# A single-token decode layer: every second weight or cache chunk, but for the last six, loaded from ScalarE's DMA queue

## The chip, the cores and the metric

The kernel runs on one core of a Trainium2 chip. The time is device microseconds (us) of one execution. Most executions of it agree within a few hundredths of a per cent: three runs lie between 229.84 and 229.97 us.

## What is computed

One token `x` (1 x 1024) goes through a layer norm; the result `xn` feeds two branches in parallel, and both are added to `x`.

- Attention with a cache: 32 query heads in 4 groups of 8, each group with its own keys and values. Of 65,536 cached positions only the last 4,096 are read.
- A gated feed-forward with 3,584 hidden columns.

```python
xn = layernorm(x)
q = (xn @ wq)                                   # 1024 -> 32 heads x 128
p = softmax(q . k_cache[last 4096] * 128**-0.5) # per head; 8 heads share one of 4 key groups
attention = (p @ v_cache[last 4096]) @ wo       # 4096 -> 1024
h = gelu(xn @ w_gate) * (xn @ w_up)             # 1024 -> 3584, tanh form of gelu
out = x + attention + h @ w_down                # 3584 -> 1024
```

All is float32. With one token there is hardly any arithmetic per weight: 94.4 MB of weights and cache are read once, and each value is used once (a key or value of the cache eight times).

## The kernel before

**Chunks.** All that is read from memory is cut into 24 chunks, listed in `items` (lines 75 to 79) in the order in which they are used:

`q0 q1 q2 q3 | k0 g0 v0 g1 g2 g3 | k1 u0 v1 u1 u2 u3 | o0 o1 o2 o3 | d0 d1 d2 d3`

The letters stand for `wq` (q), the keys (k) and values (v) of the cache, `w_gate` (g), `w_up` (u), `wo` (o) and `w_down` (d). A chunk fills a tile `chunk` of 128 partitions x 8192 floats (4 MB), or less: a chunk of q or o has one row of 32 KB for each partition, one of g or u has 28 KB for each partition, and one of k or v is two loads (two groups, the first and the second half of the tile) with 16 KB for each partition. d0 and d1 are like o; d2 is loaded in two pieces and d3, half as large, in five (`TAIL`, line 30).

**Four buffers.** The pool `stream` (line 55) has four buffers, and chunk n takes the buffer of chunk n - 4. So the load of chunk n has to wait until all engines are done with chunk n - 4. `load(n)` (line 88) issues the loads of chunk n. The first four are issued at the start; after that the main loop (line 410) works on chunk n and then calls `load(n + 4)` (line 450). All of these loads, lines 104 and 106, are issued by SyncE (SP), whose queue takes them in this order. An engine runs its instructions in the order in which the code emits them, and `manual_schedule` (line 58) leaves that order alone; a load that has to wait for its buffer therefore holds back what stands behind it on the engine that issues it.

**Work on a chunk.**
- q, g, u (`project`, line 201): the first half of each row goes through TensorE (PE, line 196), the second half through VectorE (DVE), which scales it by the token's value and adds it up in `part` (lines 184 and 186). The buffer is free when both are done.
- k (`transpose_keys` and `scores`, lines 235 and 245): for each of two groups of heads PE transposes the keys in eight groups of four blocks (line 241), ScalarE (ACT) moves each of them out of PSUM (line 242), PE forms the scores (line 250), DVE takes the maximum (line 253), and ACT the exponential (line 256). Between the two groups of k0 the queries are finished (lines 211 to 226), and between those of k1 the gelu (lines 344 to 355). The buffer is free after the last transpose of the second group.
- v (`values`, line 261): PE transposes the probabilities, ACT moves them out (line 273), PE multiplies them with the values (line 278).
- o and d (`contract`, line 393): half of the rows on PE (line 389), half on DVE (line 186); for the last chunks all on PE.

ScalarE issues two loads itself, both of `x`, at the start (lines 111 and 114); else it computes.

Of the kernel before, what the change touches and what calls it, by code (L numbers as in the profile page):

```python
# [39 lines left out]
def tile_decode_layer(  # L40
# [12 lines left out]
    nc = tc.nc  # L53
# [21 lines left out]
    items = [("q", jj) for jj in range(NJ)]  # L75
# [12 lines left out]
    def load(n):  # L88
        kind, i = items[n]
        chunk = stream.tile([P, STREAM], F32, name="chunk")  # L90
        at = 0
        for src in source[kind](i):
            size = math.prod(src.shape[1:])
            dst = chunk[:, at:at + size]
            at += size
            if len(src.shape) == 3:
                dst = dst.rearrange("p (t n) -> p t n", t=src.shape[1])
            step = TAIL.get(len(items) - 1 - n)
            if step:
                for t in range(0, src.shape[1], step):  # L100
                    cuts = 2 if n == len(items) - 1 and t == src.shape[1] - 1 else 1
                    for cut in range(cuts):
                        cols = slice(cut * D // cuts, (cut + 1) * D // cuts)
                        nc.sync.dma_start(dst[:, t:t + step, cols], src[:, t:t + step, cols])
            else:
                nc.sync.dma_start(dst, src)
        loaded[kind, i] = chunk


# [296 lines left out]
    for n in range(ahead):  # L406
        load(n)
    layer_norm()
    state = None
    for n, (kind, i) in enumerate(items):  # L410
# [38 lines left out]
        if n + ahead < len(items):  # L449
            load(n + ahead)  # L450
# [27 lines left out]
```

## Time and profile before

| | |
|---|---|
| median of 3 runs | 229.92 us (229.84 to 229.97) |
| the profiled execution | 229.72 us, of which its span is 227.9 us |
| mean granted TensorE clock | 0.79 |
| busy: PE, DVE, ACT | 54%, 43%, 15% of the span |
| DMA: q1 (SyncE's queue) | 97.1% of what 16 engines could work in the span |
| read from HBM | 94.38 MB |

The span runs from the first to the last instruction; the rest of the time, 1.8 us, lies around it. The times in the views of the trace count from the span's start. In a timeline, a row has its start, how long it takes, the engine and line, what is done, and in square brackets how long the engine had been idle and who ended that. SPq and ACTq are the instructions by which SyncE and ScalarE issue loads: what follows such a row is the issue and not the move of the data. Matmuls of float32 show as two records each.

### The profile page before, as it was taken

What the parts mean: (1) busy time and instruction counts of PE and PEld (TensorE: products, weight loads), DVE (VectorE), ACT (ScalarE), POOL (GpSimd) and SP (SyncE); (2) the same over time, 40 slices, a digit from 0 to 9 for tenths busy, and PEclk for the clock granted to TensorE, in tenths of its full rate; (3) what the DMA queues carried; (4) which work ended last, traced back from release to release, by engine and by line L of the source; (5) the groups of instructions that cost most, each with busy time, mean ns of one, the idle gap of its engine ahead of it and who ended that gap; (6) DMA issues with size and microseconds to landing.
All of it is one profiled execution on the core that took longest, in us unless ns stands there. A gap on an engine that the chain in (4) does not pass through costs nothing.

```text
span 227.9 us, 2497 instructions
## 1 busy us (share of the span) xinstructions
PE 123.2 (54%) x1096; PEld 60.6 (27%) x1096; DVE 97.0 (43%) x103; ACT 33.3 (15%) x57; POOL 0.7 (0%) x6
## 2 busy tenths in 40 slices
PE   1160622567679834269806985384875425063754
PEld 1110000144364701017305472110571202021331
DVE  7340724520204164260380227966817356292600
ACT  2000000054273400006316350000000000000000
POOL 1000000000000000000000000000000000000000
PEclk9999999599958996577975899959655556675879
DMA  7989999999999999999999999999999999999991
GB/s 277 455 380 454 460 391 443 411 456 436 393 440 461 410 410 453 401 438 451 400 428 449 428 424 441 428 443 403 440 454 405 437 449 414 431 443 391 436 378 47
DMA packets 4786, 94.53 MB, mean 415 GB/s; under 512 B 540, under 2 KB 552, under 8 KB 1192
## 3 DMA queue, kind: packets, MB, share of 16 engines
q1 hardware_dynamic: 4760, 94.38, 97.1%
q8 instruction: 8, 0.13, 0.2%
q14 instruction: 2, 0.02, 0.0%
q10 hardware_dynamic: 16, 0.01, 0.0%
HBM read 94.38 MB, written 0.00 MB: 414 GB/s over the span
## 4 chain that ended last, share of the span: by engine, by line
DMA 57%; PE 22%; DVE 11%; ACT 6%; issue 2%; SPq 0%; ACTq 0%; DVEq 0%
DMA chunk<-in_A_k_cache 23%; DMA chunk<-in_B_w_down 15%; DMA chunk<-in_A_wo 14%; PE kt_p L241 8%; DMA chunk<-in_A_wq 5%; PE o_p L278 3%; DVE part L186 3%; PE s_p L250 3%; PE out_p L389 3%; PE acc_q L196 2%; DVE out_part L186 2%; DVE m L253 2%; ACT kT L242 2%; ACT p L256 2%; ACT pT L273 1%
## 5 line engine op out<-in xcount | busy, mean ns | idle before, releaser
L186 DVE SCALAR_TENSOR_TENSOR part<-chunk,xz,part 128x3584 f32<-128x3584 f32 (+1 forms) x9 | 37.1, 4126 | 32.1 <-DMA chunk<-in_A_wq 17.8
L241 PE MATMUL kt_p<-ident,chunk 128*128 128x128 f32 x128 | 23.7, 354 | 15.9 <-ACT kT L242 13.1
L242 ACT ACTIVATE kT<-kt_p 128x512 f32<-128x512 f32 x32 | 18.2, 596 | 70.9 <-PE kt_p L241 70.9
L196 PE MATMUL acc_q<-chunk,xz 128*32 128x512 f32 x64 | 14.3, 1043 | 24.0 <-DMA chunk<-in_A_wq 24.0
L241 PEld LDWEIGHTS kt_p<-ident,chunk 128*128 128x128 f32 x128 | 18.6, 180 | 24.8 <-ACT kT L242 16.2
L389 PE MATMUL out_p<-chunk,hz 128*32 128x256 f32 x160 | 14.8, 530 | 16.5 <-DMA chunk<-in_B_w_down 16.5
L186 DVE SCALAR_TENSOR_TENSOR out_part<-chunk,oz,out_part 128x1024 f32<-128x1024 f32 x15 | 19.3, 1285 | 10.4 <-DMA chunk<-in_A_wo 10.0
L389 PE MATMUL out_p<-chunk,oz 128*32 128x256 f32 x128 | 13.1, 580 | 15.7 <-DMA chunk<-in_A_wo 15.7
L196 PE MATMUL acc_g<-chunk,xz 128*32 128x512 f32 x56 | 10.9, 817 | 11.6 <-DMA chunk<-in_B_w_gate 11.6
L253 DVE TENSOR_REDUCE m<-s_p 128x1 f32<-128x1024 f32 x4 | 4.9, 1222 | 22.0 <-PE s_p L250 22.0
L186 DVE SCALAR_TENSOR_TENSOR out_part<-chunk,hz,out_part 128x1024 f32<-128x1024 f32 x8 | 10.3, 1284 | 9.1 <-DMA chunk<-in_B_w_down 8.9
L389 PEld LDWEIGHTS out_p<-chunk,hz 128*32 128x32 f32 x160 | 6.7, 147 | 24.6 <-DMA chunk<-in_B_w_down 12.5
L196 PEld LDWEIGHTS acc_q<-chunk,xz 128*32 128x32 f32 x64 | 2.5, 159 | 34.2 <-DMA chunk<-in_A_wq 23.3
L389 PEld LDWEIGHTS out_p<-chunk,oz 128*32 128x32 f32 x128 | 5.2, 156 | 23.2 <-DMA chunk<-in_A_wo 18.5
L196 PE MATMUL acc_u<-chunk,xz 128*32 128x512 f32 x56 | 9.4, 713 | 2.6 <-DMA chunk<-in_B_w_up 2.6
L278 PE MATMUL o_p<-chunk,pT 128*32 128x128 f32 x256 | 7.8, 274 | 1.9 <-ACT pT L273 1.9
L250 PE MATMUL s_p<-kT,qz 128*32 128x512 f32 x64 | 8.7, 612 | 0.0
L184 DVE TENSOR_SCALAR part<-chunk,xz 128x3584 f32<-128x3584 f32 (+1 forms) x3 | 6.5, 2169 | 3.9 <-DMA chunk<-in_A_wq 3.9
L278 PEld LDWEIGHTS o_p<-chunk,pT 128*32 128x32 f32 x256 | 6.7, 110 | 2.9 <-ACT pT L273 2.9
L196 PEld LDWEIGHTS acc_g<-chunk,xz 128*32 128x32 f32 x56 | 2.1, 133 | 18.9 <-DMA chunk<-in_B_w_gate 14.5
L256 ACT ACTIVATE p<-s_p,negm 128x1024 f32<-128x1024 f32 x4 | 4.5, 1114 | 8.5 <-DVE negm L254 8.5
L350 DVE TENSOR_TENSOR t_sb<-g_sb 128x512 f32<-128x512 f32 (+1 forms) x2 | 1.4, 686 | 9.8 <-ACT g_sb L349 9.8
(93 smaller groups left out, 73.5 us busy)
## 6 DMA issues: line engine op xcount, KB each, us to landing
chunk<-in_A_wq SPq DMA_DIRECT2D x4, 4096.0 KB, 30.8
chunk<-in_A_wo SPq DMA_DIRECT2D x4, 4096.0 KB, 27.6
chunk<-in_B_w_gate SPq DMA_DIRECT2D x4, 3584.0 KB, 20.5
chunk<-in_B_w_up SPq DMA_DIRECT2D x4, 3584.0 KB, 16.5
chunk<-in_A_k_cache SPq DMA_DIRECT2D x4, 2048.0 KB, 28.3
chunk<-in_A_v_cache SPq DMA_DIRECT2D x4, 2048.0 KB, 28.5
chunk<-in_B_w_down SPq DMA_DIRECT2D x2, 4096.0 KB
chunk<-in_B_w_down SPq DMA_DIRECT2D x2, 2048.0 KB, 30.9
```

What stands on the lines that cost most here:

```text
L184: nc.vector.tensor_scalar(total, w, factor, None, op0=ALU.mult)
L186: nc.vector.scalar_tensor_tensor(total, w, factor, total, op0=ALU.mult, op1=ALU.add)
L196: nc.tensor.matmul(acc[kind][32 * c:32 * c + 32, b, :], z, w[:, n * NB:(n + 1) * NB], start=start, stop=stop,)
L241: nc.tensor.transpose(t_p[:, jj * P:(jj + 1) * P], kn[:, j * DH:(j + 1) * DH], ident)
L242: nc.scalar.activation(kT[:, i, :], t_p, AF.Copy)
L250: nc.tensor.matmul(s_p[32 * c:32 * c + 32, b, :], qz[:, g, :], kT[:, i, :], start=True, stop=True)
L253: nc.vector.reduce_max(m[:, g:g + 1], s_p, axis=AX.XY)
L256: nc.scalar.activation(p, s_p, AF.Exp, bias=negm[:, g:g + 1], scale=SCALE, accum_out=l[:, g:g + 1])
L273: nc.scalar.activation(pT[:, b].rearrange("p j q -> p (j q)"), t_p, AF.Copy)
L278: nc.tensor.matmul(o_p[32 * c:32 * c + 32, g, :], pT[:, b, jj, 32 * c:32 * c + 32], vn[:, j * DH:(j + 1) * DH], start=(b == 0 and jj == 0) ...
L350: nc.vector.tensor_mul(ts, gs, gs)
L389: nc.tensor.matmul(out_p[32 * c:32 * c + 32, :], z, w[:, c * CO:(c + 1) * CO], start=start, stop=stop)
```

## The change

`load` picks the issuing engine by the chunk's number: odd ones below 18 go to ScalarE. These are nine chunks: q1, q3, g0, g1, g3, u0, u1, u3 and o1. All others stay with SyncE, the last six (o2, o3 and all of d) among them. Buffers, their number, the order of work on PE and DVE, and the shapes of the loads are the same. The lines of the kernel behind the change stand two further down.

```diff
     def load(n):
         kind, i = items[n]
         chunk = stream.tile([P, STREAM], F32, name="chunk")
+
+        queue = nc.scalar if n % 2 and n < len(items) - 6 else nc.sync
...
             else:
-                nc.sync.dma_start(dst, src)
+                queue.dma_start(dst, src)
```

On SyncE, from its first load to that of `wo`: the rows before are q0 to q3, k0, g0, v0, then g1, g2 and g3, k1, u0, v1, then u1, u2 and u3, and the four of o.

```order
L106 DMA chunk<-in_A_wq 128x8192 x4
L106 DMA chunk<-in_A_k_cache 128x4096 x2
L106 DMA chunk<-in_B_w_gate 128x7168
L106 DMA chunk<-in_A_v_cache 128x4096 x2
L106 DMA chunk<-in_B_w_gate 128x7168 x3
L106 DMA chunk<-in_A_k_cache 128x4096 x2
L106 DMA chunk<-in_B_w_up 128x7168
L106 DMA chunk<-in_A_v_cache 128x4096 x2
L106 DMA chunk<-in_B_w_up 128x7168 x3
L106 DMA chunk<-in_A_wo 128x8192 x4
```

The same stretch of SyncE behind the change: q0 and q2, k0, v0, g2, k1, v1, u2, then o0, o2 and o3.

```order
L108 DMA chunk<-in_A_wq 128x8192 x2
L108 DMA chunk<-in_A_k_cache 128x4096 x2
L108 DMA chunk<-in_A_v_cache 128x4096 x2
L108 DMA chunk<-in_B_w_gate 128x7168
L108 DMA chunk<-in_A_k_cache 128x4096 x2
L108 DMA chunk<-in_A_v_cache 128x4096 x2
L108 DMA chunk<-in_B_w_up 128x7168
L108 DMA chunk<-in_A_wo 128x8192 x3
```

The key chunk k0 now follows q2 directly on SyncE's queue, and g0, which stood behind k0, is no longer on that queue.

On ScalarE, from its first load of `x` to the exponential of the second group of heads and the probabilities of v0, before:

```order
L111 DMA x_rows<-in_A_x 4x256
L114 DMA x_out<-in_A_x 4x256
L170 ACT_TABLE_LOAD
L170 ACTIVATE st<-st 128x1
L242 ACTIVATE kT<-kt_p 128x512 x8
L215 ACTIVATE q_sb<-acc_q 128x1024
L256 ACT_TABLE_LOAD
L256 ACTIVATE p,l<-s_p,negm 128x1024
L242 ACTIVATE kT<-kt_p 128x512 x8
L256 ACTIVATE p,l<-s_p,negm 128x1024
L273 ACTIVATE pT<-pt_p 128x512 x4
```

The middle and end of the same stretch behind the change, from the root of the layer norm to the keys of k1:

```order
L172 ACTIVATE st<-st 128x1
L108 DMA chunk<-in_B_w_gate 128x7168 x2
L244 ACTIVATE kT<-kt_p 128x512 x8
L217 ACTIVATE q_sb<-acc_q 128x1024
L258 ACT_TABLE_LOAD
L258 ACTIVATE p,l<-s_p,negm 128x1024
L244 ACTIVATE kT<-kt_p 128x512 x8
L258 ACTIVATE p,l<-s_p,negm 128x1024
L108 DMA chunk<-in_B_w_gate 128x7168
L275 ACTIVATE pT<-pt_p 128x512 x4
L108 DMA chunk<-in_B_w_up 128x7168 x2
L244 ACTIVATE kT<-kt_p 128x512 x8
```

The loads of g0 and g1 now stand ahead of k0's evictions, that of g3 between the exponential and the probabilities of v0, and those of u0 and u1 ahead of k1's evictions. Each waits there for its buffer.

## The prediction

> **What bounds the kernel now.** I read the page's DMA rows first: how busy the 16 DMA engines are in 40 slices, and what SyncE's queue q1 took.
>
> ```profile
> DMA  7989999999999999999999999999999999999991
> DMA packets 4786, 94.53 MB, mean 415 GB/s; under 512 B 540, under 2 KB 552, under 8 KB 1192
> q1 hardware_dynamic: 4760, 94.38, 97.1%
> ```
>
> The DMA engines work without a break from the start to the last slice. The table of busy time by stretches says it closer: first to last column the stretch, its length, PE, weight loads, DVE, ACT, POOL, granted clock, DMA share, GB/s.
>
> ```profile
> 3.50:218.00 214.50, 117.12 (x1030) 57.53 (x1030) 94.18 (x97) 32.03 (x56) 0.00 (x0) 0.79 1.00 430
> ```
>
> From 3.5 to 218 us the share is 1.00 at 430 GB/s, and no compute engine is busy for much over half of it. The chain of work that ended last, in order of time (start, length, what), has the same at both ends and in the long steps:
>
> ```profile
> 0.74 12.27 DMA chunk<-in_A_wq
> 16.84 30.20 DMA chunk<-in_A_k_cache
> 80.19 21.89 DMA chunk<-in_A_k_cache
> 218.93 5.77 PE out_p L389 x64
> 224.72 0.43 DVE y L453
> ```
>
> So the kernel is a stream of loads with a fixed start and a fixed tail. The change can alter the time in three ways only: the rate of the stream, the start or tail, or a moment in which the queues run empty. For the third I need when each load lands; PE's timeline shows that where PE waited for it.
>
> ```profile
> 22.76 3.64 PE L196 MATMUL acc_q<-chunk,xz 128*32 128x512 f32 x16 [5.98 <-DMA chunk<-in_A_wq]
> 42.20 3.63 PE L196 MATMUL acc_q<-chunk,xz 128*32 128x512 f32 x16 [6.35 <-DMA chunk<-in_A_wq]
> 47.08 1.09 PE L241 MATMUL kt_p<-ident,chunk 128*128 128x128 f32 x8 [1.26 <-DMA chunk<-in_A_k_cache]
> 88.71 3.64 PE L196 MATMUL acc_g<-chunk,xz 128*32 128x512 f32 x14 [6.74 <-DMA chunk<-in_B_w_gate]
> 97.22 3.42 PE L196 MATMUL acc_g<-chunk,xz 128*32 128x512 f32 x14 [4.88 <-DMA chunk<-in_B_w_gate]
> 102.22 1.06 PE L241 MATMUL kt_p<-ident,chunk 128*128 128x128 f32 x8 [1.58 <-DMA chunk<-in_A_k_cache]
> 142.34 1.92 PE L196 MATMUL acc_u<-chunk,xz 128*32 128x512 f32 x14 [2.28 <-DMA chunk<-in_B_w_up]
> ```
>
> q1 lands at 22.76 and q3 at 42.20, so a chunk of 32 KB rows moves in 9.72 us. g2 and g3 land at 88.71 and 97.22: 8.51 for 28 KB rows. The first half of k0 lands 4.88 after q3. The very first load took 12.27 from issue to landing for 9.72 of moving: 2.55 us is what a load costs on top when it finds the queue empty. The other half of the ledger is when SyncE could issue (start and length of the issue):
>
> ```profile
> 16.84 0.80 SPq L106 DMA_DIRECT2D chunk<-in_A_k_cache  x2
> 27.37 0.33 SPq L106 DMA_DIRECT2D chunk<-in_B_w_gate  x1
> 69.69 0.33 SPq L106 DMA_DIRECT2D chunk<-in_B_w_gate  x1
> 75.11 0.33 SPq L106 DMA_DIRECT2D chunk<-in_B_w_gate  x1
> 80.19 0.81 SPq L106 DMA_DIRECT2D chunk<-in_A_k_cache  x2
> 127.18 0.33 SPq L106 DMA_DIRECT2D chunk<-in_B_w_up  x1
> ```
>
> The margin of a load is the time from issue to landing, less 2.55 and its own move. For k0 it is 30.2 - 2.55 - 4.88 = 22.8 us, for k1 21.9 - 7.4 = 14.5. Two loads have little: those that wait for the buffer of a key chunk. g2, issued at 69.69, lands at 88.71: it could have been issued at 88.71 - 8.51 - 2.55 = 77.65, a margin of 8.0. u2, issued at 127.18, lands at 142.34, latest issue 131.28: a margin of 4.1. These margins are what the change spends.
>
> **The change part by part.** *The issues.* Nine loads leave SyncE for ScalarE. One issue there, from ScalarE's timeline, and what it will stand ahead of in the first key pass (with DVE's work on which its buffer waits):
>
> ```profile
> 0.74 0.58 ACTq L111 DMA_DIRECT2D x_rows<-in_A_x  x1
> 74.25 1.07 ACT L273 ACTIVATE pT<-pt_p 128x512 f32<-128x512 f32 x2
> ```
>
> ```profile
> 13.11 2.35 DVE L184 TENSOR_SCALAR part<-chunk,xz 128x4096 f32<-128x4096 f32 x1 [3.89 <-DMA chunk<-in_A_wq]
> 42.25 4.48 DVE L186 SCALAR_TENSOR_TENSOR part<-chunk,xz,part 128x4096 f32<-128x4096 f32 x1 [5.23 <-DMA chunk<-in_A_wq]
> 72.97 2.08 DVE L184 TENSOR_SCALAR part<-chunk,xz 128x3584 f32<-128x3584 f32 x1
> ```
>
> Nine issues at 0.58 are 5.2 us of an engine that is idle for 85% of the span. What matters is what waits behind them. q1 and q3 go out some 1.2 us after q0 and q2, with q0's 9.72 us of data to cover that. g0 and g1 stand ahead of k0's evictions: g1 waits for DVE to be done with q3, two passes of 4.48 after 42.2, so till 51.2, before k0 can land (below). g3 stands between an exponential and v0's probabilities: g0's pass on DVE ends at 75.05, plus 0.58 makes 75.6 in place of 74.25, so v0's buffer comes free 1.4 later, out of the 14.5 of k1. u3 does the same to v1, and o0 behind it has as good a cover. u0 and u1 stand ahead of k1's evictions: u1 waits for g3's pass on DVE, 4 us after g3 has landed, and k1 lands later than that (below, with 1.5 to spare). After o1 nothing follows on ScalarE. So I take 0 for all of these; without the cover each would cost the 1.4, and u1's wait would go straight into the release of k1.
>
> *Start and tail.* The first load stays SyncE's first, the last six stay in one queue in the old order: 0.
>
> *The rate.* No row of before has two queues at work with large loads. Bounds come from what a load costs apart from its bytes:
>
> ```profile
> chunk<-in_A_wq SPq DMA_DIRECT2D x4, 4096.0 KB, 30.8
> chunk<-in_B_w_gate SPq DMA_DIRECT2D x4, 3584.0 KB, 20.5
> ```
>
> 512 KB more take 9.72 - 8.51 = 1.21 us, which is 433 GB/s; at that rate 4096 KB are 9.68 us, so a chunk has 0.04 us that isn't bytes. For 24 chunks that is 1.0 us: the most that a second queue could hide, and about what it would add if each change of queue cost as much again. From -1.0 to +1.0; I take 0, since DMA engines with a share of 1.00 have nothing else to give.
>
> *The order of arrival.* This is the real edit. With one queue a chunk gets all engines until it has landed. With two, a chunk shares them with the one that is in the other queue. How, no row shows outright, but the page's count tells what a packet is: 4760 packets in q1, of which about 540 are tiny, leaves 4220, and 33 loads of 128 rows are 4224. A packet is one partition's row. I take it that the engines serve the two queues packet by packet in turn. The Trainium skill says so too (page "DMA: Bandwidth & Descriptors", section "Queues, rings and completion order"): each engine goes round between the queues that have work, a whole packet at a time.
>
> First key pass, by hand. q0 and q1 move together and land at about 22.7, q2 and q3 at about 42.2, where q3 landed before. q0's buffer comes free 3.7 later (26.5), q1's when DVE is through both (22.8 + 2.35 + 4.48 = 29.6): k0 and g0 are queued well before 42. Then the first half of k0 (128 rows of 16 KB) takes turns with g0 (128 rows of 28 KB): both need 4.88 + 8.51 = 13.4 us and land at 55.6, not at 47.1. If the turns were equal bytes, the half would land at 42.2 + 2 x 4.88 = 52.0. The second half of k0 then pairs with g1 and lands at 69.0. Before, the buffer was free 69.69 - 47.08 = 22.6 us after the first half had landed:
>
> ```profile
> 52.18 1.93 PE L196 MATMUL acc_q<-part,unit 128*32 128x512 f32 x16
> 64.09 5.58 PE L241 MATMUL kt_p<-ident,chunk 128*128 128x128 f32 x24 [3.58 <-ACT kT L242]
> ```
>
> The second half's transposes began in earnest at 64.09, 17.0 after that landing, so at 72.6 now: the half that lands at 69.0 is in time. So g2 is issued at 55.6 + 22.6 = 78.2, against the limit of 77.65. With eight chunks moved and no ninth in either queue, the engines run dry for **0.6 us**.
>
> How sure is 22.6? It holds two stretches of transposes, one at full clock and one at half:
>
> ```profile
> 48.00:52.00 4.00, 3.35 (x26) 2.50 (x24) 0.00 (x0) 3.22 (x7) 0.00 (x0) 1.00 1.04 445
> 64.00:68.00 4.00, 3.91 (x18) 3.31 (x19) 0.00 (x0) 2.42 (x6) 0.00 (x0) 0.50 1.06 451
> ```
>
> At half clock six groups took 5.58, 0.93 each; at full clock eight took 52.2 - 47.1 = 5.1, 0.64 each. The second stretch at full clock gives back 1.7 (nothing runs dry), the first at half clock adds 2.3 (2.9 dry). So 0 to 2.9, and 0.6 as the profile stands.
>
> Second key pass. g3 can be issued at 75.1 + 8.5 = 83.6, a little later by ScalarE's wait, say 84.5; until then g2 moves alone from about 79.5, 5.0 of its 8.5. The other 3.5 alternate with g3 and end at 91.5. k1 is issued at 80.2 + 8.5 + 1.4 = 90.1. What is left of g3 (5.0, 75 rows) pairs with 75 rows of k1 (2.9): 99.4. The other 53 rows of k1's first half pair with u0: 2.0 + 3.5, to 104.9, and about 1.2 to landing makes 106.1, 3.9 later than 102.2. g3 has landed by 100.6, so its DVE pass ends at 104.6 and u1's wait is over. u2 is issued 3.9 later than 127.18, at 131.1; its limit has moved with the first stall to 131.9. It holds, by 0.8: 0.
>
> *Sum.* 0 (issues) + 0 (ends) + 0 (rate) + 0.6 (dry at g2) + 0 (at u2). The profiled execution took 229.72 for a span of 227.9; it would become 230.3. It lies 0.2 below the median of the runs, 229.92, which becomes **230.5**, slower by 0.26%. Differences under 0.2%, 0.46 us, can't be told from none on this kernel.
>
> **The rivals.**
>
> *A. No change, 229.9: k0 lands early enough.* One mechanism, at g2's issue: it needs k0's first half to land before 77.65 - 22.6 = 55.05 instead of 55.6, or half a microsecond off the release. Equal bytes in turn give 52.0, g2 at 74.6 and 3 us to spare; service in the order of issue gives 47.1 and the old program, and then the second queue does nothing at all. For it: the distance is 0.55 us and half-clock transposes alone are 1.7. Against it: a packet is a row in this trace. A turn of a whole load on each engine would have the same end: k0's first half would move next after q3 and land near 48, g2 at 70.6, 229.9. The Trainium skill (page "DMA: Bandwidth & Descriptors", section "Queues, rings and completion order") gives typical packets of 9 to 17 descriptors, by which the eight rows of an engine and the completion would be one packet; the count of 4760 speaks against that here. The Trainium skill (same page, section "Issuing engines are not separate DMA queues") states that several issuing engines save only issue time, since all loads run on the same 16 DMA engines; that would be 229.9 too, and the trace, with a share of 1.00, agrees as far as the rate goes.
>
> *B. Clearly slower, 232.8: the throttle falls on the first half of k0's transposes,* now that two chunks of q are worked on back to back just before. Price 2.9 us at g2; from 0.8 on a like delay in k1's pass runs the queue dry a second time. For it: the clock is at 0.50 in one of the two stretches already. Against: it stood at 1.00 in the first.
>
> *C. Faster, 228.9: two queues hide what a load costs apart from its bytes,* 1.0 us, and the dry moment stays small. For it: the share of 1.00 counts that cost as work. Against: 0.04 us a chunk is little enough to be no gap at all.
>
> **How the numbers follow.** Forecast (dry at g2 alone) 0.40, with 230.4 to 231.6 as its own range; A 0.32; B 0.13; C 0.15. Faster is C: 0.15. Within 0.2% is A and 0.05 of the forecast's low end: 0.37. Slower is the rest of the forecast and B: 0.48. The range takes in C's full gain and B's price: 228.9 to 232.8; beyond it I leave a second dry moment and a gain over the bound.
>
> **What would show it.** In the changed profile q0 should land near 22.7 and k0's first half near 55.6 (near 52 or 47: the service is another, and A follows). g2's issue near 78.2, with a slice of DMA share under 9 between 78 and 81 us, g2 landing later than 88.71 by what is lost; none at 132. The share of q1 and ScalarE's queue together should stay at 97 less that. I am wrong if the share stays whole from 3.5 us to the tail and the time moves all the same, or if a gap stands elsewhere.

## The result and the profile after

| | before | changed |
|---|---|---|
| median of 6 runs | 229.79 us | 235.74 us |
| lowest to highest | 229.66 to 229.97 | 233.84 to 236.81 |
| span of the profiled execution | 227.9 | 235.0 |

The ratio is 1.025, with a 95% interval from 1.0233 to 1.0268: slower by 5.95 us where 0.6 was forecast, and outside the range. The changed kernel also spreads ten times as wide, and its runs follow the granted TensorE clock: 233.84 us at 0.816, 234.62 at 0.802, and 235.74 to 236.81 at 0.757 to 0.768. The profile below is that of the slowest of the six.

The page of the changed kernel, from its part on slices and its part on queues:

```profile
PEclk9999875575976789957597589995596785575879
DMA  7999999999999699999999879999999999999990
GB/s 268 447 446 435 396 441 443 429 432 427 417 418 435 240 413 449 406 434 425 438 426 425 375 245 434 434 418 440 446 438 424 421 424 435 441 446 388 417 353 22
q1 hardware_dynamic: 3464, 59.77, 60.5%
q10 hardware_dynamic: 1312, 34.61, 34.2%
```

The engines ran dry twice: the slices with 240 and 245 GB/s. The table by stretches of the changed kernel puts bounds on them (last two columns: DMA share, GB/s).

```profile
3.50:76.00 72.50, 33.25 (x167) 14.75 (x168) 21.14 (x32) 11.21 (x18) 0.00 (x0) 0.79 1.00 430
74.00:84.00 10.00, 9.75 (x62) 5.94 (x60) 2.83 (x3) 4.85 (x9) 0.00 (x0) 0.75 0.80 310
82.00:130.00 48.00, 26.98 (x262) 15.10 (x256) 21.41 (x18) 11.36 (x19) 0.00 (x0) 0.79 1.00 428
130.00:142.00 12.00, 10.46 (x62) 6.20 (x62) 3.25 (x3) 6.09 (x12) 0.00 (x0) 0.71 0.82 320
140.00:222.00 82.00, 45.20 (x501) 22.47 (x502) 49.50 (x46) 3.58 (x7) 0.00 (x0) 0.73 1.00 430
```

Outside the two stretches the rate is that of before, 428 to 430. What a stretch lost is its length times the missing share of 430: (430 - 310) / 430 x 10 = 2.8 us in the first, (430 - 320) / 430 x 12 = 3.1 in the second. (The share column would give less: rows that are just starting count as busy, and the microsecond from 80 to 81 has a share of 1.79 at 459 GB/s.) That is 5.9 of the 7.1 us between the two profiled executions. Of the other 1.2, some 0.2 lie in the 428 from 82 to 130 us and 0.3 in the last matmuls (6.07 us in place of 5.77); the rest is not placed.

Both stretches end with SyncE's issue of a chunk that waits for a key chunk's buffer. From SyncE's timeline of the changed kernel: k0, g2, k1, u2.

```profile
24.06 0.80 SPq L108 DMA_DIRECT2D chunk<-in_A_k_cache  x2
79.20 0.33 SPq L108 DMA_DIRECT2D chunk<-in_B_w_gate  x1
92.57 0.80 SPq L108 DMA_DIRECT2D chunk<-in_A_k_cache  x2
136.47 0.33 SPq L108 DMA_DIRECT2D chunk<-in_B_w_up  x1
```

g2 goes out at 79.20 (before 69.69), u2 at 136.47 (127.18). Why so late, PE's timeline tells: q0 to q3 as they land, the first half of k0, the scores of the first group, and the first half of k1.

```profile
20.37 3.64 PE L198 MATMUL acc_q<-chunk,xz 128*32 128x512 f32 x16 [12.81 <-DMA chunk<-in_A_wq]
27.70 3.61 PE L198 MATMUL acc_q<-chunk,xz 128*32 128x512 f32 x16 [3.70 <-DMA chunk<-in_A_wq]
39.70 3.64 PE L198 MATMUL acc_q<-chunk,xz 128*32 128x512 f32 x16 [8.38 <-DMA chunk<-in_A_wq]
44.72 3.64 PE L198 MATMUL acc_q<-chunk,xz 128*32 128x512 f32 x16 [1.37 <-DMA chunk<-in_A_wq]
53.40 6.76 PE L243 MATMUL kt_p<-ident,chunk 128*128 128x128 f32 x32 [5.04 <-DMA chunk<-in_A_k_cache]
65.51 3.50 PE L252 MATMUL s_p<-kT,qz 128*32 128x512 f32 x16
110.93 6.89 PE L243 MATMUL kt_p<-ident,chunk 128*128 128x128 f32 x32 [4.75 <-DMA chunk<-in_A_k_cache]
```

k0's first half lands at 53.40 in place of 47.08, k1's at 110.93 in place of 102.22. From 53.40 to g2's issue are 25.8 us where the kernel before took 22.6.

### The profile page after: what moved, and what is told of

The parts are those of the page before. It is cut to its first block, busy times and chain, and to the rows that moved or that the text cites. A ratio compares the mean times of both kernels' runs of the same rounds, so it can differ in the third digit from the quotient of the medians.

```text
span 235.0 us, 2499 instructions
## 1 busy us (share of the span) xinstructions
PE 127.8 (54%) x1096; PEld 64.2 (27%) x1096; DVE 96.9 (41%) x103; ACT 34.2 (15%) x57; POOL 0.7 (0%) x6
## 4 chain that ended last, share of the span: by engine, by line
DMA 55%; PE 25%; DVE 13%; ACT 4%; issue 2%; ACTq 0%; SPq 0%; DVEq 0%
DMA chunk<-in_A_k_cache 20%; DMA chunk<-in_B_w_down 14%; DMA chunk<-in_A_wo 12%; PE kt_p L243 10%; DMA chunk<-in_A_wq 8%; DVE out_part L188 4%; PE o_p L280 4%; PE s_p L252 3%; PE out_p L391 3%; PE acc_q L198 2%; DVE m L255 2%; DVE part L188 2%; DVE part L186 1%; ACT pT L275 1%; PE q_p L221 1%
## 5 line engine op out<-in xcount | busy, mean ns | idle before, releaser
L243 PE MATMUL kt_p<-ident,chunk 128*128 128x128 f32 x128 | 26.8, 390 | 21.9 <-DMA chunk<-in_A_k_cache 12.7
L243 PEld LDWEIGHTS kt_p<-ident,chunk 128*128 128x128 f32 x128 | 21.2, 201 | 32.2 <-ACT kT L244 12.5
L244 ACT ACTIVATE kT<-kt_p 128x512 f32<-128x512 f32 x32 | 18.9, 597 | 75.1 <-PE kt_p L243 74.8
L198 PE MATMUL acc_q<-chunk,xz 128*32 128x512 f32 x64 | 14.5, 1058 | 26.3 <-DMA chunk<-in_A_wq 26.3
L391 PE MATMUL out_p<-chunk,oz 128*32 128x256 f32 x128 | 11.0, 503 | 12.4 <-DMA chunk<-in_A_wo 12.4
L198 PE MATMUL acc_g<-chunk,xz 128*32 128x512 f32 x56 | 9.3, 711 | 6.4 <-DMA chunk<-in_B_w_gate 6.4
L198 PEld LDWEIGHTS acc_q<-chunk,xz 128*32 128x32 f32 x64 | 2.5, 155 | 36.7 <-DMA chunk<-in_A_wq 18.7
L280 PE MATMUL o_p<-chunk,pT 128*32 128x128 f32 x256 | 9.4, 308 | 4.4 <-ACT pT L275 4.4
L252 PE MATMUL s_p<-kT,qz 128*32 128x512 f32 x64 | 10.4, 723 | 0.0
L391 PEld LDWEIGHTS out_p<-chunk,oz 128*32 128x32 f32 x128 | 4.6, 139 | 19.2 <-DMA chunk<-in_A_wo 15.4
L280 PEld LDWEIGHTS o_p<-chunk,pT 128*32 128x32 f32 x256 | 8.1, 123 | 5.4 <-ACT pT L275 5.4
```

The lines of the kernel that those rows point to most:

```text
L198: nc.tensor.matmul(acc[kind][32 * c:32 * c + 32, b, :], z, w[:, n * NB:(n + 1) * NB], start=start, stop=stop,)
L243: nc.tensor.transpose(t_p[:, jj * P:(jj + 1) * P], kn[:, j * DH:(j + 1) * DH], ident)
L244: nc.scalar.activation(kT[:, i, :], t_p, AF.Copy)
L252: nc.tensor.matmul(s_p[32 * c:32 * c + 32, b, :], qz[:, g, :], kT[:, i, :], start=True, stop=True)
L280: nc.tensor.matmul(o_p[32 * c:32 * c + 32, g, :], pT[:, b, jj, 32 * c:32 * c + 32], vn[:, j * DH:(j + 1) * DH], start=(b == 0 and jj == 0) ...
L391: nc.tensor.matmul(out_p[32 * c:32 * c + 32, :], z, w[:, c * CO:(c + 1) * CO], start=start, stop=stop)
```

## The experiments

The theories. 1, turns: a key chunk shares the engines with a neighbour, lands late, its buffer comes free late, and both queues run dry. 2, waits: ScalarE's issues wait for buffers and hold back what ScalarE has to do behind them (the hold). 3, clock: TensorE's half clock, brought on by work that comes bunched, lengthens the key passes. Each diff below is against the changed kernel, or against the kernel before where that is said. Medians stand beside 229.81 to 229.84 for the kernel before on the same chip.

### The odd chunks issued by GpSimd

```diff
-        queue = nc.scalar if n % 2 and n < len(items) - 6 else nc.sync
+        queue = nc.gpsimd if n % 2 and n < len(items) - 6 else nc.sync
```

> The nine odd chunks are issued by GpSimd, which does nothing else in this kernel after its start, so that no issue stands ahead of ScalarE's work. Theory 1 (turns: a key chunk shares the DMA engines with its neighbour, lands late, its buffer comes free late, and both queues run dry): as the changed kernel, 234 to 237 us, DMA share well under 1 near 78 us and near 135 us. Theory 2 (waits: ScalarE's issues wait for buffers and hold back the evictions behind them): 229.8 to 230.3, no dry stretch. Theory 3 (clock: TensorE's half clock alone lengthens the key passes): no view of where loads are issued; 229.8 if the matmuls arrive as before, else as theory 1.

233.0 us, ratio 1.013 (1.0095 to 1.0166). The stretches, from its table:

```profile
74.00:84.00 10.00, 9.23 (x78) 5.54 (x80) 3.60 (x4) 5.67 (x10) 0.00 (x0) 0.87 0.87 343
130.00:142.00 12.00, 11.05 (x185) 7.26 (x183) 3.37 (x3) 5.16 (x10) 0.53 (x1) 0.95 1.02 434
```

The time lies between what theories 1 and 2 expected, and neither will do alone: the first stretch is there with nothing ahead of ScalarE's work (2.0 us lost), and the second is gone.

### ScalarE's waits without the sharing

Against the kernel before.

```diff
+        odd = n % 2 and n < len(items) - 7
...
-                nc.sync.dma_start(dst, src)
+                first = 32 if odd else 0
+                if odd:
+                    nc.scalar.dma_start(dst[:, :first], src[:, :first])
+                nc.sync.dma_start(dst[:, first:] if odd else dst, src[:, first:] if odd else src)
```

> Of each odd chunk but o1 ScalarE loads only the first 32 columns (128 bytes for each partition), and SyncE the rest: ScalarE keeps the issues with their waits ahead of its evictions, while the bytes stay in one queue. Theory 1: 229.8 to 230.5 (the small rows may cost some tenths), k0's first half lands near 47. Theory 2: 233 to 237, with evictions late behind the issues. Theory 3: 229.8 to 230.5.

230.68 us, ratio 1.0038 (1.0025 to 1.0051), 0.2 above the range of theory 1, with no dry stretch: g2 is issued at 71.10, u2 at 126.17. v0's probabilities do start late, at 76.94, and k1 is issued at 84.50 in place of 80.19, and no queue runs empty for it. The 0.9 us lie at least in part in the rate, 425 GB/s from 84 to 148 us: 64 us at 1.2% less than 430 are 0.7. So the waits alone open no dry stretch, as long as the loads come in the old order.

### Only g0 and u0 on ScalarE, and all but g0 and u0

```diff
-        queue = nc.scalar if n % 2 and n < len(items) - 6 else nc.sync
+        queue = nc.scalar if n in (5, 11) else nc.sync
```

> Only g0 and u0, the chunks behind k0 and k1, go to ScalarE. Theory 1: g0 gets in ahead of k0, k0's first half lands near 55.6 (47.1 + 8.5), k1's near 110, and both stretches run dry: 233 to 236. Theory 2: two issues whose buffers are free long before ScalarE has evictions to do, so 229.8 to 230.2.

240.65 us, ratio 1.047 (1.0438 to 1.0506), well above the 233 to 236 of theory 1: two chunks in the second queue do more harm than nine. g0 finds that queue empty and takes turns with q2 and q3. PE's timeline of this kernel, q3 and k0's first half:

```profile
50.77 3.64 PE L198 MATMUL acc_q<-chunk,xz 128*32 128x512 f32 x16 [12.46 <-DMA chunk<-in_A_wq]
55.66 5.12 PE L243 MATMUL kt_p<-ident,chunk 128*128 128x128 f32 x24 [1.25 <-DMA chunk<-in_A_k_cache]
```

q3 is late by 50.77 - 42.20 = 8.6 us, which is g0's whole move (8.51), and k0 with it: 55.66, as forecast for the pair. The landing was right and its price too low: by the rate the first stretch lost 5.0 us here (215 GB/s from 74 to 84) and the second 6.4 (276 from 130 to 148).

```diff
-        queue = nc.scalar if n % 2 and n < len(items) - 6 else nc.sync
+        queue = nc.scalar if n % 2 and n < len(items) - 6 and n not in (5, 11) else nc.sync
```

> The changed kernel, but g0 and u0 stay with SyncE, behind k0 and k1; seven chunks are on ScalarE. Theory 1: k0's first half lands by 50, k1's by 104, nothing or little runs dry: 229.8 to 231. Theory 2: the waits of g1, g3, u1 and u3 on ScalarE are as in the changed kernel: 233 to 236.

229.90 us, ratio 1.0005 (0.9995 to 1.0014). With g0 and u0 back behind the key chunks all is as before, though seven chunks and four of the waits are on ScalarE. k0's first half is there at 47.81, g2 goes out at 73.19, and k1's first half is there at 102.27. Theory 1 holds; theory 2 alone is out.

### Only the first four

```diff
-        queue = nc.scalar if n % 2 and n < len(items) - 6 else nc.sync
+        queue = nc.scalar if n in (1, 3, 5, 7) else nc.sync
```

> Only q1, q3, g0 and g1 go to ScalarE; from g2 on all is SyncE's. Theory 1 (turns): the first dry stretch of the changed kernel as it is there, near 78 us, the second gone: 232 to 233.3. If the first stretch were made up for later: 229.8 to 230.5.

232.67 us, ratio 1.011 (1.0078 to 1.0142): the first stretch is there alone and is not made up for later. g2 goes out at 78.65, and 336 GB/s between 74 and 84 are 2.2 us lost; the median is 2.9 longer, and the other 0.7 is not placed.

### Shorter rows on ScalarE's queue

```diff
-                queue.dma_start(dst, src)
+                cuts = 4 if queue is nc.scalar and len(src.shape) == 2 else 1
+                for cut in range(cuts):
+                    cols = slice(cut * size // cuts, (cut + 1) * size // cuts)
...
+                        queue.dma_start(dst[:, cols], src[:, cols])
```

> The changed kernel, but each load on ScalarE (o1 apart) is cut into four loads of a quarter of the columns, so that its rows are 7 or 8 KB. Theory 1 with turns of one row each: the key chunk's rows of 16 KB now get two thirds of the engines, its first half lands near 50 in place of 53.4, and the dry stretches shrink or go: 229.8 to 232.5. If the queues shared by bytes, nothing changes: 234 to 237. Theory 2 (waits on ScalarE, now four issues each behind one wait): 234 to 238.

247.52 us, ratio 1.076, against the expectation. ScalarE's timeline says why: the eight issues of g0 and g1, and the first eviction.

```profile
39.81 24.52 ACTq L114 DMA_DIRECT2D chunk<-in_B_w_gate  x8
64.37 1.08 ACT L250 ACTIVATE kT<-kt_p 128x512 f32<-128x512 f32 x2 [42.13 <-DMA chunk<-in_B_w_gate]
```

With four loads for each chunk ScalarE's issues wait for earlier loads to land, 24.5 us for eight, and hold the first eviction to 64.37; the eight of q1 and q3 took 18.7 (from 1.98) and held the root of the layer norm from 7.79 to 22.04. On the turns it says this much: PE starts k0's transposes at 49.33, before which the half has landed, so shorter rows in the other queue did bring it 4 us forward. On the time it is no test of them.

### TensorE idle until the keys come

```diff
-        blocks(kind, xz[:, 0, jj, :], w[:, :n], count, jj == 0, False)
+        if kind != "q" or jj == 0:
+            blocks(kind, xz[:, 0, jj, :], w[:, :n], count, jj == 0, False)
```

> The changed kernel without TensorE's half of the query projection for q1, q2 and q3 (left out, so that TensorE is idle until the keys come); loads as in the changed kernel. Theory 3 (half clock lengthens the key pass): the clock is 1.00 in k0's first transposes, k0's buffer comes free some 23 us after its first half has landed in place of 25.8, the first dry stretch is all but gone: 231 to 233.5. If the clock has no part: 234 to 237, with 25 us or more.

235.58 us, the median without the longest run, ratio 1.023 (1.0169 to 1.0286): no gain. The page is that of the longest, 237.99 us; PE's busy slices stand over the clock (5.9 us each):

```profile
PE   1105000009784969260971696836449854161783
PEclk9999855555976779957697587985987575755589
```

The clock falls to half from the sixth slice on, while PE has nothing to do from 24 to 53 us, and is still there when the keys arrive; k0's buffer comes free 26.1 us after its first half has landed (53.38, 79.43). Bunched matmuls are not what lowers it: that part of theory 3 falls. It fell while PE had nothing to do; the end of the point-by-point part comes back to this.

### g3 and u3 back to SyncE

```diff
-        queue = nc.scalar if n % 2 and n < len(items) - 6 else nc.sync
+        queue = nc.scalar if n % 2 and n < len(items) - 6 and n not in (9, 15) else nc.sync
```

> The changed kernel, but g3 and u3, whose issues stand between an exponential and the probabilities on ScalarE, are issued by SyncE; g0 and u0 stay with ScalarE. Theory 1 alone: both dry stretches stay, 234 to 237. Theories 1 and 2 together (the hold delays v0's release, then k1's load, then the second stretch): the first dry stretch as in the changed kernel, the second gone or small: 232 to 233.5, as with GpSimd.

239.67 us, ratio 1.043 (1.038 to 1.0479), beyond both. With g3 gone the second queue is empty when u0 comes (issued at 90.98), and u0 gets in ahead of g3 and k1, as g0 did above. PE's timeline, k1's first half:

```profile
113.29 6.88 PE L243 MATMUL kt_p<-ident,chunk 128*128 128x128 f32 x32 [4.54 <-DMA chunk<-in_A_k_cache]
```

It took away the hold and made the order worse at once; the next one takes away the hold alone.

### The same queues without the hold

```diff
+        if n in (6, 12):
+            load(n - 1 + ahead)
-        if n + ahead < len(items):
+        if n + ahead < len(items) and n not in (5, 11):
             load(n + ahead)
```

> The changed kernel with the issues of g3 and u3 on ScalarE placed behind the probabilities of v0 and v1 in place of ahead of them: the same chunks in the same queues, without the hold. If the hold is what made the second stretch run dry: v0's buffer comes free near 89 in place of 92.6, k1's first half lands near 107 in place of 110.9, the second stretch is gone or under 1 us, 232.5 to 233.5, as with GpSimd. If the hold has no part: both stretches as in the changed kernel, 234.5 to 236.5.

232.82 us, ratio 1.0123 (1.0085 to 1.016). SyncE's issues of g2, k1 and u2, and PE at k1's first half:

```profile
79.26 0.33 SPq L108 DMA_DIRECT2D chunk<-in_B_w_gate  x1
89.76 0.81 SPq L108 DMA_DIRECT2D chunk<-in_A_k_cache  x2
131.64 0.33 SPq L108 DMA_DIRECT2D chunk<-in_B_w_up  x1
```

```profile
107.45 6.00 PE L243 MATMUL kt_p<-ident,chunk 128*128 128x128 f32 x32
```

The first stretch is as in the changed kernel, the second is gone (428 GB/s from 130 to 142). So the hold is worth 2.9 us here, though only on top of the turns: with the old order of arrival it opened no dry stretch. Not all of it is the wait itself: k1 goes out 2.8 us earlier than in the changed kernel, of which 1.15 are the wait and 1.6 the first matmuls on v0, which ran at half clock behind the wait (3.53) and at full clock here (1.96). With the same wait they ran at half clock in the run with the small loads (3.44) and at full clock in the one with all but g0 and u0 (1.95).

### One queue, the release of k0's buffer delayed

Against the kernel before: transposes of k0's blocks that nobody reads, behind its last ones (24, then 52).

```diff
             nc.scalar.activation(kT[:, i, :], t_p, AF.Copy)
+        if g == 1:
+            t_p = small("kt_p")
+            for j in range(52):
+                nc.tensor.transpose(t_p[:, (j % 4) * P:(j % 4 + 1) * P], kn[:, (j % 32) * DH:(j % 32 + 1) * DH], ident)
         keys[g] = kT
```

> The kernel before, one queue, with 24 more transposes of k0's blocks on TensorE after its last ones, so that nothing but the release of k0's buffer is late. By the rule read from the runs so far (what is lost is the time by which g2's issue is later than 76.3 us): g2's issue at 73 to 75.5, nothing lost, 229.7 to 230.1. If any delay of that release cost time: 233 to 235.

> The same with 52 more transposes: g2's issue at 77 to 82, and the time lost is that issue less 76.3 to within 0.7 us: 230.5 to 235.5, with one dry stretch before 84 us and none near 135 us. By the limit of the prediction, 77.65, it would be 1.3 us less.

With 24 g2 goes out at 72.30, 0.7 before the expected span, and the time is 229.92 (ratio 1.001, 0.9999 to 1.0021). With 52 it is 232.54 (1.0102, 1.0072 to 1.0131); SyncE's timeline and the table of that kernel:

```profile
78.92 0.33 SPq L106 DMA_DIRECT2D chunk<-in_B_w_gate  x1
```

```profile
74.00:84.00 10.00, 9.48 (x83) 6.43 (x81) 3.12 (x3) 1.65 (x4) 0.00 (x0) 1.00 0.81 314
```

Lost in the stretch: (430 - 314) / 430 x 10 = 2.7 us; by the rule 78.92 - 76.3 = 2.6; in the median 2.7. The first stretch of the changed kernel is made here with a single queue, by the late issue alone. By the prediction's limit, 77.65, it would have cost 1.3.

### Only u0

```diff
-        queue = nc.scalar if n % 2 and n < len(items) - 6 else nc.sync
+        queue = nc.scalar if n == 11 else nc.sync
```

> Only u0 goes to ScalarE, nothing else. Turns of rows, with an empty second queue: u0 gets in ahead of k1 whole, k1's first half lands at 102.2 + 8.5 = 110.7, u2 is issued near 135.7, 5.3 us after the limit of 130.4 read from the runs so far: 234.4 to 236, first stretch full, second dry. If the order of arrival were not what counts: 229.8.

235.78 us, ratio 1.0269 (1.0244 to 1.0295). PE at k1's first half, and the second stretch:

```profile
110.63 1.06 PE L243 MATMUL kt_p<-ident,chunk 128*128 128x128 f32 x8 [1.35 <-DMA chunk<-in_A_k_cache]
```

```profile
130.00:142.00 12.00, 11.36 (x130) 7.48 (x128) 3.37 (x3) 5.74 (x11) 0.00 (x0) 0.85 0.73 287
```

k1's half lands where 102.2 + 8.5 puts it. In this profile, of the fastest of its four runs, u2 goes out at 134.09, earlier than forecast; the rule gives 3.7 us, the table 4.0, and the run is 4.9 longer than the median before.

### The rule over all runs

g2's issue, GB/s from 74 to 84 us, what that lost, and the issue less 76.3:

| kernel | issue | GB/s | lost | issue - 76.3 |
|---|---|---|---|---|
| GpSimd | 78.38 | 343 | 2.0 | 2.1 |
| first four | 78.65 | 336 | 2.2 | 2.4 |
| g3, u3 on SyncE | 78.78 | 321 | 2.5 | 2.5 |
| one queue, 52 transposes | 78.92 | 314 | 2.7 | 2.6 |
| changed | 79.20 | 310 | 2.8 | 2.9 |
| without the hold | 79.26 | 304 | 2.9 | 3.0 |
| PE idle | 79.43 | 298 | 3.1 | 3.1 |
| g0 and u0 only | 80.98 | 215 | 5.0 | 4.7 |

76.3 was fitted to these, apart from the 52 transposes and the kernel without the hold, whose expectations were written with it. Three with issues of 71.10, 72.30 and 73.19 lost no time there. One limit and one price, 1 us for each us, hold, to within 0.3 us, for kernels that come by a late issue in different ways. No version here beats the kernel before: its two issues, at 69.69 and 127.18, are early enough.

## Why the prediction was wrong, point by point

*What bounds the kernel, and the kind of loss:* right. The rate did not change (430), and start and tail hardly. The first place, g2's issue, was right; u2's issue was named as the next to fail and put at nothing. The sizes were wrong at both, by the terms below.

*Turns of rows:* right. A row takes 1.215 us on its engine for q (9.72 / 8), 1.064 for g and 0.61 for k. k0 starts when q2 is through (landed 39.70), and q3 lands 5.02 later; in that time 5.02 / (1.215 + 0.61) = 2.75 rows of k0's first half went on each engine, in turn with as many of q3. The other 5.25 go in turn with g0: 5.25 x (1.064 + 0.61) = 8.8, so 53.5; measured 53.40. The packets that the trace keeps say the same: from the first to the last of the 128 rows of this half, 44 rows of q3 and 92 of g0 were begun. By equal bytes it would have been 39.7 + 2 x 4.88 = 49.5. The Trainium skill's rule (page "DMA: Bandwidth & Descriptors", section "Queues, rings and completion order"), turns between queues by packet, agrees with that, with a packet of one row. The forecast of 55.6 was 2.2 too late, since q2 got through 5 us before q3: SyncE's queue had a start (the first row of q0 moved at 1.76, that of q1 at 6.21).

*"So g2 is issued at 55.6 + 22.6 = 78.2":* 79.20, by two errors that nearly cancel. The landing was 2.2 early, the release took 25.8 in place of 22.6. Half clock on k0's first transposes, rival B's mechanism, came true: 6.76 in place of 5.1. That the scores between the two groups would run at half clock as well was not in it: 3.50, where the chain of the kernel before has

```profile
57.63 1.90 PE s_p L250 x16
```

Together 1.7 + 1.6 = 3.3, all of the difference of 3.2.

*"Against the limit of 77.65 ... dry for 0.6 us":* failed, by more than the issue did. Even for 78.2 the rule gives 1.9. The step that failed is the 2.55 us that a load costs on top when it finds the queue empty: it was read from the kernel's very first load, and in mid-stream it is more. In the kernel with 52 transposes g2 goes out at 78.92 into an empty queue, with nothing beside it, and PE gets it here:

```profile
91.28 1.92 PE L196 MATMUL acc_g<-chunk,xz 128*32 128x512 f32 x14 [0.23 <-DMA chunk<-in_B_w_gate]
```

That is 12.36 us from issue to landing: 3.85 on top of the move of 8.51. Put in place of 2.55 it makes the limit 88.71 - 12.36 = 76.35, the one that was fitted. In three other runs in which g2 followed a dry stretch alone (only the first four, g3 and u3 on SyncE, g0 and u0 only) it took 12.25 to 12.80. The landings in the trace show where the difference comes from: 15 of the 16 DMA engines were done with g2 11.05 us after its issue, as 2.55 would have it, and the last one 1.26 later, while the first load's 16 landed within 0.7 of each other. Why one engine is late stays open. So the margins that I put at 8.0 and 4.1 were 6.6 and 3.4 (for u2, 136.47 less the 2.8 and 3.1 lost in the changed kernel is 130.6; the expectation of the last run has 130.4).

*"It holds, by 0.8: 0", at u2:* failed; 3.1. k1's first half was to land at 106.1 and landed at 110.93. The first step that broke it is "v0's buffer comes free 1.4 later, out of the 14.5 of k1". ScalarE's and PE's timelines of the changed kernel around it: the exponential, the issue of g3, v0's probabilities, and the first matmuls on v0.

```profile
82.65 1.11 ACT L258 ACTIVATE p<-s_p,negm 128x1024 f32<-128x1024 f32 x1 [2.85 <-DVE negm L256]
84.62 0.33 ACTq L108 DMA_DIRECT2D chunk<-in_B_w_gate  x1
85.00 1.09 ACT L275 ACTIVATE pT<-pt_p 128x512 f32<-128x512 f32 x2 [1.15 <-issue]
```

```profile
85.65 3.53 PE L280 MATMUL o_p<-chunk,pT 128*32 128x128 f32 x64 [1.90 <-ACT pT L275]
```

The wait itself was sized well (1.15), but the matmuls behind it fell into half clock (3.53, where the second set took 1.96), and k0's buffer had come free 1.0 later than forecast; so k1 went out at 92.57, 2.5 later than I had. The second step is the start of a load beside another that is under way. I had k1 move from 91.5, 1.4 after its issue; by the trace's packets its first row moved at 96.02, 3.45 after it, and that of g3 3.60 after its own issue, where g2's, on idle engines, took 0.97. In most other such starts of these runs it was 3.1 to 3.9, in one 1.7. These 2.5 and 2.0 are 4.5 of the 4.8 by which k1 landed late. And the cover was not one: 14.5 us is how long k1's load could be put off before a single queue runs dry. With two queues each us by which it joins late lets another row of the neighbour go first. Issued 2.8 us earlier, without the hold, it landed 3.5 us earlier (107.45 against 110.93), and the second stretch was gone.

*Rivals.* B was nearest, in mechanism and time (232.8), but it had k1's pass as an afterthought, and the range left a second dry moment out by name. A, no change, needed k0's half by 55.05, and got 53.40: it came to pass and did not help, since the release and the limit were both off. The trace agrees with the Trainium skill's rule that several issuing engines save only issue time (page "DMA: Bandwidth & Descriptors", section "Issuing engines are not separate DMA queues") as far as the rate goes: 430 GB/s before, 428 to 430 outside the dry stretches. The loss lies in the order of arrival and in what waited for it.

*What sets the half clock* is answered in part. The traces keep the granted clock in pieces of 3.41 us. Over all 14 traces PE had been busy for 0.33 of the piece ahead of one at half clock, and for 0.89 of the piece ahead of one at full clock. So it is idling that goes ahead of half clock, and chunks that land in pairs leave longer gaps: PE had idled for 5.04 and 4.75 us when the two key passes of the changed kernel began at half clock, and for 1.26 and 1.58 when those of the kernel before began at full clock. About one piece in eight does not fit, and no run takes the idling away alone, so this is a pattern and not a test. Why six runs of the changed kernel spread over 3 us stays open.

## What to carry to other kernels

When loads already keep the DMA engines full, a second queue moves nothing faster; it changes who arrives first, and a chunk whose buffer is held long must not share its turn with one that is needed later. Before moving a load, write down for each issue how long it could be put off until the engines have nothing left, and spend from the smallest margin. What a load costs on an empty queue has to be read in mid-stream: here 3.85 us, where the kernel's first load gave 2.55. A margin that was read with one queue is no cover with two.

## What the hardware showed that was not expected

- A chunk in an otherwise empty second queue gets in ahead: one of 28 KB rows put off what stood in the first queue by its whole move (q3 by 8.6 us, k1 by 8.4), so two chunks alone (240.65 us) cost more than nine (235.74).
- GpSimd's queue takes turns as ScalarE's does: k0's first half landed at 53.57 and at 53.40.
- The granted clock fell to 0.5 while TensorE was idle, between 24 and 53 us of the kernel without most of the query projection.
- In the changed kernel the first row of a load moved 0.97 us after its issue when the engines were idle (g2), and 3.45 and 3.60 after it when they were at work on the other queue (k1, g3).
- Eight issues on ScalarE took 24.5 us when each chunk was cut in four, against 17.3 for the two uncut issues, and ended waiting for a load of their own.
